# Loading the last weight matrix in pieces of 18, 6, 6, 4, 1 and 1 rows, and turning the last head's output ahead of the first piece's matmuls

## The chip, the cores and the metric

The kernel runs on one core of a Trainium2 chip. The metric is the device time of one execution in microseconds (us). Executions of the kernel before took 211.63 to 211.93 us in three runs, with a median of 211.7.

## The reference, cut to what matters

```python
def reference(A_x, A_k_cache, A_v_cache, A_wq, A_wo, B_x, B_w1, B_w2, B_w3, B_w4):
    # A: attention, one query token, 4 batches, 32 heads on 16 K/V heads, last 2048 keys, head size 128
    # ... q = xn @ wq, softmax, p @ v ...   then  o.reshape(B, 1, 4096) @ wo
    # B: an MLP. With one token, the shifted part of it contributes nothing but padding, so x1 = x:
    # h2 = gelu(layernorm(x1) @ w3) @ w4       w3: 576 x 4608, w4: 4608 x 576
    # B returns xn + h2; the whole result is 4 x 1 x 576
    ...
    xn = _layernorm(x, axis=-1)
    return x + _A_ref(xn, A_k_cache, A_v_cache, A_wq, A_wo) + _B_ref(xn, B_w1, B_w2, B_w3, B_w4)
```

The change touches the last product of each half: `gelu(...) @ w4`, and `o @ wo` for the last four K/V heads.

## The kernel before

Everything is read once from HBM in one queue, in the order wq, K and V of head after head (with wo and w3 between), and w4 last. w4 has 4608 rows; the kernel lays them out as 36 "rows" of 128 partitions by 576 columns and loads them in six pieces, each a DMA of its own with its own semaphore, so that matmuls of one piece can start while the next is on its way (in the trace of before rows 10 to 17 start at 202.05 us, and the next piece lands at 204.55).

```python
    W4_PIECES = [0, 10, NFH, NF - 6, NF - 2, NF - 1, NF]      # NF = 36, NFH = 18: 10, 8, 12, 4, 1, 1 rows

    def load_w4():
        t = wp.tile([P, NF, D], BF16, tag="w", name="w4_sb")
        for lo, hi in zip(W4_PIECES, W4_PIECES[1:]):
            e = lo // NFH
            src = B_w4[e * (F // 2):(e + 1) * (F // 2), :].rearrange("(p i) n -> p i n", i=NFH)
            nc.sync.dma_start(out=t[:, lo:hi, :], in_=src[:, lo - e * NFH:hi - e * NFH, :])
        w_tiles["w4"] = t
```

The results of both halves add up in one PSUM tile, `acc`. In the tail every second term goes to a second tile, `acc_odd`, at partitions from QD = 32 on, so that two matmuls stream at once (in the timeline the two of a pair start within 0.01 us of each other; those of a single row, both into `acc`, start 0.12 us apart):

```python
    def acc_matmuls(terms):
        for i in range(NI):                                   # NI = 2 halves of 288 columns
            for n, (lhsT, rhs) in enumerate(terms):
                to, q, start = (second[0], QD, second[1]) if second and n % 2 else (acc, 0, False)
                nc.tensor.matmul(out=to[q:q + OR, :], lhsT=lhsT[:, NI - 1 - i:NI - 1 - i + OR],
                                 rhs=rhs[:, i * CW:(i + 1) * CW], start=start, stop=False, skip_group_check=True)
                # ...

    def mlp_out(lo, hi):
        w4 = w_tiles["w4"]
        for i in range(lo, hi, 2):
            acc_matmuls([(gT[:, u, :], w4[:, u, :]) for u in range(i, min(i + 2, hi))])
```

The tail, in the order of TensorE's program. `o_turn` transposes a head's output on TensorE, `o_sum` folds it on VectorE, `o_spread` is eight small matmuls, `o_pick` two VectorE instructions, `o_proj` 16 matmuls with wo:

```python
    for s in range(NSL):
        pv(hl, s)
    o_scale(hl)                      # ScalarE, 0.69 us
    o_turn(hl - 1)
    o_sum(hl - 1)
    # ...
    mlp_out(*pieces[0])
    o_turn(hl)
    o_sum(hl)
    o_spread(hl)
    o_pick(hl)
    mlp_out(*pieces[1])
    o_proj(hl)
    mlp_out(*pieces[2])
    mlp_out(*pieces[3])
    second.clear()
    odd = const.tile([OR, CW], F32)
    nc.scalar.activation(out=odd[:], in_=acc_odd[QD:QD + OR, :], func=ACT.Copy)
    seen = const.tile([1, 1], F32)
    nc.vector.tensor_copy(out=seen[:], in_=odd[0:1, 0:1])
    for lo, hi in pieces[4:]:        # the two single rows, into acc alone
        mlp_out(lo, hi)
    fin = const.tile([OR, CW], out.dtype)
    nc.vector.tensor_tensor(out=fin[:], in0=acc[0:OR, :], in1=odd[:], op=ALU.add)
    nc.sync.dma_start(out=o2.rearrange("b (i n) -> (b i) n", i=NI), in_=fin[:])
```

## Time and profile before

| | before |
|---|---|
| time, median of the first 3 runs | 211.7 us |
| span of the profiled run | 209.8 us |
| DMA rate over the span | 416 GB/s |
| chain of waits: DMA, TensorE | 73%, 17% |
| last piece of w4 landed | 206.67 us |
| store of the result issued | 207.72 us |

In all views PE is TensorE, PEld its weight loads, DVE VectorE, ACT ScalarE, POOL GpSimd, and SP the engine that issues the DMAs (SPq its queue). The first lines are from the page of the kernel before: the span in 40 slices with the granted TensorE clock in tenths, the DMA engines' busy share in tenths and their rate; then the chain of waits by engine.

```profile
PEclk9999589696997556958999979997999985969999
DMA  8999999999999999999999999999999999999991
GB/s 301 400 419 431 434 428 419 439 428 425 445 429 427 423 431 425 449 419 431 440 422 434 434 409 444 434 428 423 444 414 437 418 450 419 434 428 421 434 409 69
...
DMA 73%; PE 17%; DVE 7%; ACT 1%; issue 1%; SPq 0%; DVEq 0%
```

The DMA engines are busy 90% or more of every slice from the second to the last but one. From this I took it, as an estimate, that a change that moves no bytes can act only after the last K/V work, in the final 10 us. Next, the DMA issues of that stretch (window 165 to 210 us): size, and time from issue to landing.

```profile
w_sb<-in_B_w_dram SPq DMA_DIRECT2D x1, 1728.0 KB, 34.6
w_sb<-in_B_w_dram SPq DMA_DIRECT2D x1, 1440.0 KB, 29.2
w_sb<-in_B_w_dram SPq DMA_DIRECT2D x1, 1152.0 KB, 31.3
w_sb<-in_B_w_dram SPq DMA_DIRECT2D x1, 576.0 KB, 31.2
w_sb<-in_B_w_dram SPq DMA_DIRECT2D x2, 144.0 KB, 24.4
```

All are issued 22 to 35 us before they land; the queue, not the issue, decides when: the last three are issued 4.85 and 4.90 us apart and land 0.35 and 0.37 us apart. With the issue times (168.4 to 184.5 us) the pieces land at 197.61, 200.35, 204.55, 205.95, 206.30 and 206.67 us. TensorE meets them like this (timeline: start, duration, engine and line, what; in brackets idle time and what ended it; most of the alternating matmuls left out):

```profile
199.41 0.29 PE L183 MATMUL acc<-w_sb,gT 128*8 128x288 bf16 x1
...
200.74 0.66 PE L403 MATMUL oT<-ident_w,O_sb 128*128 128x128 f32 x4
...
201.77 0.35 PE L422 MATMUL R<-on,sel_wo 128*128 128x32 bf16 x8 [0.38 <-DVE on L413]
...
203.10 0.29 PE L183 MATMUL acc<-wo_sb,op 128*8 128x288 bf16 x1
...
203.96 0.29 PE L183 MATMUL acc<-wo_sb,op 128*8 128x288 bf16 x1
...
204.59 0.28 PE L183 MATMUL acc<-w_sb,gT 128*8 128x288 bf16 x1 [0.34 <-DMA w_sb<-in_B_w_dram]
...
206.55 0.65 PE L183 MATMUL acc<-w_sb,gT 128*8 128x288 bf16 x4
206.75 0.40 ACT L606 ACTIVATE odd<-acc_odd 8x288 f32<-8x288 f32 x1 [7.07 <-PE acc_odd L183]
...
207.72 0.36 SPq L614 DMA_DIRECT2D out_dram<-fin  x1
```

Ten rows, the turn, a short wait for VectorE's sum, the spread, eight rows, the projection; then a wait of 0.34 us for the 12-row piece (the line at 204.59), and from there 18 rows in a row. Two rows take 0.24 us (two pairs, 0.12 us from start to start), a single one 0.24 too, as it has no partner.

### The profile page before, as it was taken

What the parts mean: (1) busy time and instruction counts of PE and PEld (TensorE: products, weight loads), DVE (VectorE), ACT (ScalarE), POOL (GpSimd) and SP (SyncE); (2) the same over time, 40 slices, a digit from 0 to 9 for tenths busy, and PEclk for the clock granted to TensorE, in tenths of its full rate; (3) what the DMA queues carried; (4) which work ended last, traced back from release to release, by engine and by line L of the source; (5) the groups of instructions that cost most, each with busy time, mean ns of one, the idle gap of its engine ahead of it and who ended that gap; (6) DMA issues with size and microseconds to landing.
All of it is one profiled execution on the core that took longest, in us unless ns stands there. A gap on an engine that the chain in (4) does not pass through costs nothing.

```text
span 209.8 us, 2403 instructions
## 1 busy us (share of the span) xinstructions
PE 149.1 (71%) x955; PEld 62.7 (30%) x955; DVE 120.4 (57%) x217; ACT 33.9 (16%) x64; POOL 2.8 (1%) x15
## 2 busy tenths in 40 slices
PE   0287496869691009659899599967994926989884
PEld 0133132223240003214364144332532401425353
DVE  3741899584840082825706878985399571771420
ACT  7602201020220000202102121120111110202300
POOL 4010000000000000000000000000000000000000
PEclk9999589696997556958999979997999985969999
DMA  8999999999999999999999999999999999999991
GB/s 301 400 419 431 434 428 419 439 428 425 445 429 427 423 431 425 449 419 431 440 422 434 434 409 444 434 428 423 444 414 437 418 450 419 434 428 421 434 409 69
DMA packets 6659, 87.32 MB, mean 416 GB/s; under 512 B 748, under 2 KB 1016, under 8 KB 1400
## 3 DMA queue, kind: packets, MB, share of 16 engines
q1 hardware_dynamic: 6640, 87.17, 97.5%
q8 instruction: 7, 0.11, 0.2%
q10 hardware_dynamic: 8, 0.00, 0.1%
q14 instruction: 4, 0.03, 0.0%
HBM read 87.17 MB, written 0.00 MB: 415 GB/s over the span
## 4 chain that ended last, share of the span: by engine, by line
DMA 73%; PE 17%; DVE 7%; ACT 1%; issue 1%; SPq 0%; DVEq 0%
DMA w_sb<-in_B_w_dram 33%; DMA vn<-in_A_v_cache_dram 24%; DMA wo_sb<-in_A_wo_dram 10%; DMA wq_sb<-in_A_wq_dram 6%; PE S L338 6%; DVE kt L225 4%; PE acc L183 3%; PE g_ps L456 2%; PE q_ps L285 2%; PE O L390 1%; PE oT L403 1%; DVE qz L317 1%; PE gT_ps L468 1%; DVE mx L344 1%; ACT q_sb L296 1%
## 5 line engine op out<-in xcount | busy, mean ns | idle before, releaser
L225 DVE STREAM_TRANSPOSE kt<-kn 128x1024 int32<-128x1024 int32 x64 | 76.5, 1216 | 12.4 <-DMA kn<-in_A_k_cache_dram 12.1
L338 PE MATMUL S<-kt,qz 128*128 128x512 bf16 x256 | 78.9, 437 | 3.1 <-DVE kt L225 3.1
L390 PE MATMUL O<-vn,PT 128*32 128x512 bf16 x256 | 27.2, 425 | 39.9 <-DMA vn<-in_A_v_cache_dram 38.1
L338 PEld LDWEIGHTS <-qz 128*128 128x128 bf16 x256 | 21.6, 103 | 41.1 <-issue 25.1
L366 ACT ACTIVATE E<-S 128x512 bf16<-128x512 f32 x16 | 9.6, 597 | 122.4 <-PE S L360 122.4
L390 PEld LDWEIGHTS <-PT 128*32 128x32 bf16 x256 | 7.2, 94 | 48.1 <-issue 29.6
L372 DVE STREAM_TRANSPOSE PT<-E 128x512 bf16<-128x512 bf16 x16 | 11.4, 710 | 15.3 <-ACT E L366 15.2
L397 ACT ACTIVATE O_sb<-O,rd 128x512 f32<-128x512 f32 x16 | 11.0, 686 | 15.8 <-issue 11.0
L356 DVE TENSOR_REDUCE nm<-mg 8x1 bf16<-8x16 f32 x16 | 2.4, 151 | 19.0 <-PE mg L351 19.0
L413 DVE TENSOR_REDUCE on<-oT 128x8 bf16<-128x128 f32 x16 | 4.5, 279 | 13.4 <-PE oT L403 13.4
L344 DVE TENSOR_REDUCE mx<-S 128x1 f32<-128x512 f32 x16 | 10.5, 657 | 1.3 <-PE S L338 1.3
L403 PE MATMUL oT<-ident_w,O_sb 128*128 128x128 f32 x64 | 11.2, 304 | 0.0
L403 PEld LDWEIGHTS oT<-ident_w,O_sb 128*128 128x128 f32 x64 | 9.1, 159 | 5.0 <-issue 3.2
L183 PE MATMUL acc<-wo_sb,op 128*8 128x288 bf16 x56 | 7.5, 286 | 0.0
L376 PEld LDWEIGHTS dn<-rs,same_j 128*128 128x128 f32 x32 | 5.8, 188 | 2.9 <-ACT E L366 0.7
L360 PE MATMUL S<-nm,j_row 8*128 8x512 bf16 x16 | 6.4, 402 | 0.0
L329 PE MATMUL S<-negbig,ohT 4*128 4x512 bf16 x16 | 6.2, 385 | 0.0
L183 PE MATMUL acc<-w_sb,gT 128*8 128x288 bf16 x38 | 5.1, 286 | 0.3 <-DMA w_sb<-in_B_w_dram 0.3
L183 PEld LDWEIGHTS <-op 128*8 128x8 bf16 x64 | 4.6, 87 | 2.5 <-issue 0.7
L351 PE MATMUL mg<-dm,sel_jb 128*8 128x16 bf16 x16 | 2.8, 174 | 3.6 <-DVE dm L346 3.5
L351 PEld LDWEIGHTS <-sel_jb 128*8 128x8 bf16 x16 | 1.3, 83 | 12.3 <-issue 5.6
L474 DVE COPY g_x<-gT_ps 128x64 f32<-128x64 f32 (+1 forms) x3 | 0.6, 193 | 7.7 <-PE gT_ps L468 7.7
(93 smaller groups left out, 84.6 us busy)
## 6 DMA issues: line engine op xcount, KB each, us to landing
kn<-in_A_k_cache_dram SPq DMA_DIRECT2D x16, 2048.0 KB, 22.0
vn<-in_A_v_cache_dram SPq DMA_DIRECT2D x16, 2048.0 KB, 24.4
wo_sb<-in_A_wo_dram SPq DMA_DIRECT2D x4, 1152.0 KB, 24.4
w_sb<-in_B_w_dram SPq DMA_DIRECT2D x1, 4608.0 KB, 34.0
wq_sb<-in_A_wq_dram SPq DMA_DIRECT2D x1, 4096.0 KB, 12.8
w_sb<-in_B_w_dram SPq DMA_DIRECT2D x1, 1728.0 KB, 34.6
w_sb<-in_B_w_dram SPq DMA_DIRECT2D x1, 1440.0 KB, 29.2
w_sb<-in_B_w_dram SPq DMA_DIRECT2D x2, 576.0 KB, 32.9
```

The source lines that it names most:

```text
L183: nc.tensor.matmul(out=to[q:q + OR, :], lhsT=lhsT[:, NI - 1 - i:NI - 1 - i + OR], rhs=rhs[:, i * CW:(i + 1) * CW], start=start, stop=False ...
L225: nc.vector.transpose(out=kt[:], in_=src)
L329: nc.tensor.matmul(out=S_ps[h][:].rearrange("p (c k) -> p c k", k=QD), lhsT=ohT[:], rhs=negbig[:].unsqueeze(1).to_broadcast([B, SC, QD]), ...
L338: nc.tensor.matmul(out=S_ps[h][:], lhsT=qz[:, z0:z0 + P], rhs=kt[:, ib, :, e:2 * QD:2].rearrange("p c k -> p (c k)"), start=False, stop=Fa ...
L344: nc.vector.reduce_max(out=mx[:], in_=S_ps[h][:], axis=AX.X)
L360: nc.tensor.matmul(out=S_ps[h][:], lhsT=j_row[:], rhs=st.pop(("nm", h))[:, 0:1].to_broadcast([NJ, NW]), start=False, stop=False, skip_grou ...
L366: nc.scalar.activation(out=E[h][:].rearrange("p c k -> p (c k)"), in_=S_ps.pop(h)[:], func=ACT.Exp, scale=scale, accum_out=rs[:])
L372: nc.vector.transpose(out=PT[h][:], in_=E.pop(h)[:])
L376: nc.tensor.matmul(out=dn[:], lhsT=same_j[:], rhs=st.pop(("rs", h))[:], start=True, stop=True)
L390: nc.tensor.matmul(out=O_ps[h][g * QD:(g + 1) * QD], lhsT=PT[h][:, c, :], rhs=vn[:, :, c, :], start=(s == 0), stop=False, skip_group_check ...
L397: nc.scalar.activation(out=O_sb[h][:], in_=O_ps.pop(h)[:], func=ACT.Copy, scale=st.pop(("rd", h))[:, 0:1])
L403: nc.tensor.transpose(out=oT[:, s, :], in_=o[:, s, :], identity=ident_w[:, s * NJ:s * NJ + P])
```

## The change

The intent is to fill the wait at 204.59. The first two pieces become one, the 12-row piece becomes two of six, so that rows 18 to 23 arrive on their own; and the last head's chain of turn, sum, spread and pick starts before the first piece's matmuls, so that VectorE's part hides behind 18 rows instead of 8.

```diff
-    W4_PIECES = [0, 10, NFH, NF - 6, NF - 2, NF - 1, NF]
+    W4_PIECES = [0, NFH, NF - 12, NF - 6, NF - 2, NF - 1, NF]
@@
-    mlp_out(*pieces[0])
     o_turn(hl)
     o_sum(hl)
     o_spread(hl)
     o_pick(hl)
+    mlp_out(*pieces[0])
+    o_proj(hl)
     mlp_out(*pieces[1])
-    o_proj(hl)
     mlp_out(*pieces[2])
     mlp_out(*pieces[3])
```

## The prediction

> **What bounds the kernel now.** The loads. The page's slices show the DMA engines at 0.8 or more up to the last slice, 416 GB/s over the span; [...] 429 GB/s in the stretch 170 to 190 us. The chain of waits is 73% DMA. The change moves no byte and adds no load: six pieces of w4 before, six after, issued by SP between 168.4 and 184.5 us, over 20 us before they land. Only the tail after about 199 us can change.
>
> **The tail before.** Issue times (timeline) plus times to landing (DMA issues) give the landings of the pieces (10, 8, 12, 4, 1, 1 rows): 197.6, 200.4, 204.55, 205.95, 206.3, 206.65 us. In the timeline TensorE runs ten rows at 199.41, turns the last head at 200.74, waits for VectorE's sum, starts the spread at 201.77, eight rows at 202.05, the projection at 203.10. It waits 0.3 us for the 12-row piece and starts it at 204.59, then streams 12+4+1+1 rows: two rows cost 2 x 0.12 us, a single row 0.24. Row 34 starts at 206.55, the last matmul near 206.9. Then ScalarE's copy (0.40), VectorE's probe and sum (0.14 + 0.43), the store at 207.72.
>
> **What the change does, costed.**
> 1. The turn comes first. It waits for ScalarE's scaled output (199.00 to 199.69), so it starts near 199.75, not 200.74. TensorE idles 0.3 us more there; turn to spread stays 1.03 us (spread near 200.8).
> 2. The 18 rows (landed by about 200.4) run from 201.1 to 203.25 (9 x 0.24 us), hiding VectorE's pick. Projection to about 204.25, as before.
> 3. Rows 18 to 23 land on their own by about 202.5 (estimate: half way between 200.4 and 204.55) and fill the wait, 204.25 to 205.0. Rows 24 to 29 (landed 204.55) run to 205.7. TensorE is about 0.35 us ahead.
> 4. But the 4-row piece still lands at 205.95: a new wait of about 0.25 us. Its rows take 0.48 us; row 34 starts near 206.47, row 35, whose piece lands at 206.65, near 206.72.
>
> So of 0.35 us won on TensorE about 0.08 survives; the last landings take the rest. Packets per load stay 128; one took 520 ns at 13,824 bytes and 178 at 4,608, so about 7 ns is fixed, and their number doesn't change: the last landing should not move.
>
> **Predicted time:** 211.6 us, against 211.7; 211.1 to 212.2 should hold it 8 times in 10 (the three runs before spread over 0.3). Faster by over 2%: 0.5%; within 2%: 99%; slower by over 2%: 0.5%.
>
> **What would show it.** Right: the turn near 199.75, spread near 200.8, no DMA wait before rows 18 to 29, a new TensorE wait of 0.1 to 0.4 us for the 4-row piece, the last piece landing within 0.3 us of 206.65, ScalarE's copy of the odd half 0 to 0.15 us earlier. Step 2 is wrong if TensorE waits for the 18-row piece; step 3 if the wait stands before rows 18 to 23; step 4 if row 34 starts over 0.2 us earlier.
>
> **What would make it wrong.** The last landings moving with the sizes ahead of them: [...] the postings for one piece spread over 1.8 us. If packet sizes change how far the slowest engine lags, the end moves by tenths of a microsecond either way. A lower granted clock in the tail (1.00 now) would add some.

## The result, and the profile after

| | runs | median | range | ratio to before, 95% interval |
|---|---|---|---|---|
| before | 6 | 211.75 us | 211.63 to 211.93 | |
| after | 6 | 211.93 us | 211.62 to 212.26 | 1.0007 (0.9993 to 1.0021) |

A ratio is the mean time of one kernel's runs over that of the other's of the same rounds, so it is not quite the ratio of the medians. The time is the same. The six runs of after fall into two groups: 211.62, 211.62, 211.70 and 212.16, 212.20, 212.26. The trace is of a run of the lower group.

The same lines of the page, after:

```profile
PEclk9999589696969556958999979997999985969999
DMA  7999999999999999999999999999999999999991
GB/s 301 400 412 437 428 428 428 436 422 428 469 408 420 433 428 427 438 431 428 431 437 428 422 425 446 425 425 436 422 436 428 421 435 440 425 425 448 418 402 72
...
DMA 72%; PE 18%; DVE 6%; ACT 1%; issue 1%; SPq 0%; DVEq 0%
```

The stream of loads is as it was. The issues (same window; the two six-row pieces share a line of 864 KB):

```profile
w_sb<-in_B_w_dram SPq DMA_DIRECT2D x1, 2592.0 KB, 31.9
w_sb<-in_B_w_dram SPq DMA_DIRECT2D x2, 864.0 KB, 33.9
w_sb<-in_B_w_dram SPq DMA_DIRECT2D x1, 576.0 KB, 31.1
w_sb<-in_B_w_dram SPq DMA_DIRECT2D x2, 144.0 KB, 24.4
```

The pieces land at 200.48, 202.55, 204.61, 206.00, 206.41 and 206.78 us: the boundary at row 18 and those from row 30 on are where they were, within 0.13 us. And TensorE's tail (timeline, same columns):

```profile
199.81 0.66 PE L403 MATMUL oT<-ident_w,O_sb 128*128 128x128 f32 x4 [0.26 <-ACT O_sb L397]
...
200.85 0.35 PE L422 MATMUL R<-on,sel_wo 128*128 128x32 bf16 x8 [0.38 <-DVE on L413]
...
201.13 0.29 PE L183 MATMUL acc<-w_sb,gT 128*8 128x288 bf16 x1
...
203.34 0.29 PE L183 MATMUL acc<-wo_sb,op 128*8 128x288 bf16 x1
...
204.32 0.29 PE L183 MATMUL acc<-w_sb,gT 128*8 128x288 bf16 x1
...
205.05 0.29 PE L183 MATMUL acc<-w_sb,gT 128*8 128x288 bf16 x1
...
205.66 0.29 PE L183 MATMUL acc<-w_sb,gT 128*8 128x288 bf16 x1
...
206.04 0.28 PE L183 MATMUL acc<-w_sb,gT 128*8 128x288 bf16 x1
...
206.53 0.70 PE L183 MATMUL acc<-w_sb,gT 128*8 128x288 bf16 x4
206.74 0.40 ACT L606 ACTIVATE odd<-acc_odd 8x288 f32<-8x288 f32 x1 [6.98 <-PE acc_odd L183]
...
207.74 0.37 SPq L614 DMA_DIRECT2D out_dram<-fin  x1
```

Rows 18 to 23 run at 204.32 and rows 24 to 29 at 205.05, without a wait. The last pair of row 29 starts at 205.66 and a pair takes 0.12, so the next could start near 205.79; the four-row piece starts at 206.04. That is the new wait, 0.25 us. The bracket shows none at 206.04, because each of these matmuls is recorded with 0.29 us, although the next pair starts 0.12 us after it. Counted from start to start in the same way, the wait before was not 0.34 but 0.51 us (the last pair of the projection starts at 203.96, so the next could start at 204.08). The chain of waits in order of time (start, duration, link) says it plainly. Before:

```profile
169.92 34.62 DMA w_sb<-in_B_w_dram
204.55 0.04 issue
204.59 0.28 PE acc L183
```

and after:

```profile
174.94 31.06 DMA w_sb<-in_B_w_dram
206.00 0.04 issue
206.04 0.28 PE acc L183
```

The last DMA of the chain was the 12-row piece, issued at 169.92; now it is the four-row piece, issued at 174.94. Row 34 starts at 206.53 instead of 206.55, the store at 207.74 instead of 207.72. The wait has moved 1.45 us towards the end, and nothing came out at the end.

### The profile page after: what moved, and what is told of

It is laid out like the page before. It is cut to its first block, busy times and chain, and to the rows that moved or that the text cites. A ratio compares the mean times of both kernels' runs of the same rounds, so it can differ in the third digit from the quotient of the medians. Undisturbed runs are those within 1.5% of the kernel's fastest.

```text
span 209.8 us, 2403 instructions
## 1 busy us (share of the span) xinstructions
PE 149.9 (71%) x955; PEld 62.8 (30%) x955; DVE 120.4 (57%) x217; ACT 33.9 (16%) x64; POOL 2.8 (1%) x15
## 4 chain that ended last, share of the span: by engine, by line
DMA 72%; PE 18%; DVE 6%; ACT 1%; issue 1%; SPq 0%; DVEq 0%
DMA vn<-in_A_v_cache_dram 35%; DMA w_sb<-in_B_w_dram 31%; PE S L338 7%; DMA wq_sb<-in_A_wq_dram 6%; DVE kt L225 3%; PE acc L183 2%; PE g_ps L456 2%; PE q_ps L285 2%; PE O L390 2%; PE oT L403 1%; DVE qz L317 1%; PE gT_ps L468 1%; DVE mx L344 1%; PE S L360 1%; ACT q_sb L296 1%
## 5 line engine op out<-in xcount | busy, mean ns | idle before, releaser
L338 PE MATMUL S<-kt,qz 128*128 128x512 bf16 x256 | 79.7, 441 | 3.1 <-DVE kt L225 3.1
L338 PEld LDWEIGHTS <-qz 128*128 128x128 bf16 x256 | 21.7, 104 | 41.5 <-issue 25.8
```

Of the source, the lines that this page charges most:

```text
L338: nc.tensor.matmul(out=S_ps[h][:], lhsT=qz[:, z0:z0 + P], rhs=kt[:, ib, :, e:2 * QD:2].rearrange("p c k -> p (c k)"), start=False, stop=Fa ...
```

## The experiments

Theory T: the landings of the last pieces set the end; what TensorE wins earlier, it waits away there. Rivals: the amount of TensorE's work in the tail is the bound; or the new order costs what the new sizes win. Kernels of one table shared a chip and the runs of before.

| kernel | runs (us) | median | ratio to before, 95% interval |
|---|---|---|---|
| before | 11: 211.51 to 211.81, one 212.28 | 211.71 | |
| e1_after_again | 211.58, 212.46, 211.43, 211.76, 211.44, 211.68 | 211.63 | 0.9999 (0.9983 to 1.0014) |
| e2_order_only | 211.77, 211.59, 212.39, 211.59, 211.64, 211.56 | 211.62 | 1.0000 (0.9985 to 1.0015) |
| e3_sizes_only | 214.15, 213.90, 213.89, 212.82, 212.28, 212.24 | 213.35 | 1.0069 (1.0040 to 1.0098) |
| e8_split_four | 211.95, 212.65, 212.73, 211.60, 211.81, 212.71 | 212.30 | 1.0023 (1.0004 to 1.0042) |

| kernel | runs (us) | median | ratio to before, 95% interval |
|---|---|---|---|
| before | 11: 211.53 to 211.94 | 211.71 | |
| e4_after_no_proj | 211.40, 211.51, 211.65, 211.41, 211.77 | 211.51 | 0.9993 (0.9981 to 1.0004) |
| e5_before_no_proj | 213.10, 213.97, 211.67, 211.72, 211.62, 214.00 | 212.41 | 1.0046 (1.0009 to 1.0083) |
| e6_after_no_last6 | 211.73, 212.87, 213.11, 212.94, 211.76, 211.98 | 212.43 | 1.0039 (1.0019 to 1.0059) |
| e7_before_no_last6 | 212.76, 212.29, 212.29, 212.47, 212.42 | 212.42 | 1.0035 (1.0023 to 1.0047) |

| kernel | runs (us) | median | ratio to before, 95% interval |
|---|---|---|---|
| before | 11: 211.50 to 211.90 | 211.68 | |
| e9_filled | 211.62, 211.63, 211.77, 211.76, 211.56 | 211.63 | 1.0000 (0.9988 to 1.0011) |
| e10_after_third | 213.12, 211.71, 211.56, 212.41, 211.48, 211.44 | 211.63 | 1.0002 (0.9988 to 1.0016) |
| e11_filled_again | 211.54, 211.56, 211.75, 211.60, 211.49 | 211.56 | 0.9996 (0.9984 to 1.0008) |
| e12_after_fourth | 211.80, 211.48, 211.73, 211.82, 211.48 | 211.73 | 0.9999 (0.9987 to 1.0011) |

The first run of each list is the profiled one.

### e1_after_again: the control

No edit.

> The changed kernel again, as the control of this chip. Theory T (the landings of the last pieces set the end, and what TensorE wins earlier is spent waiting for them): ratio to before within 0.9990 to 1.0025, no DMA wait of TensorE before rows 18 to 29, one of 0.2 to 0.4 us before the four-row piece. The first result had runs at 211.6 to 211.7 and others at 212.2 to 212.3 us; if those two levels are of the kernel, they come again in this kernel and not in before; if of the chip or of chance, before or the other kernels of this call show them too.

Measured: ratio 0.9999; TensorE's tail as in the first trace, the last piece landed at 206.73 and the store left at 207.71. One run of six was at 212.46, and one of the eleven of before at 212.28. The high level is not of this kernel alone, but it is more frequent here; more below.

### e2_order_only: the new order, the old sizes

```diff
 # against after
-    W4_PIECES = [0, NFH, NF - 12, NF - 6, NF - 2, NF - 1, NF]
+    W4_PIECES = [0, 10, NFH, NF - 6, NF - 2, NF - 1, NF]
```

> New order of TensorE's work, old sizes (10, 8, 12, 4, 1, 1). T: the turn near 199.8 and the spread near 200.85 as in the changed kernel, but the wait stays before the twelve-row piece (about 0.3 us, landing near 204.55), the rest of the tail as before; ScalarE's copy of the odd half at 206.75 within 0.1 us, time within 0.1 us of before. Rival (the new idle time ahead of the turn, 0.26 us, is what cancels a gain): slower than before by 0.2 to 0.3 us.

Measured: ratio 1.0000. The interval reaches to 0.3 us slower, so the time alone does not exclude the rival's 0.2 to 0.3; the trace does, for this run: the idle time ahead of the turn (0.26 us) comes before a wait of 1.67 us, and row 34 and the store follow the landing of the 12-row piece as in before. But two numbers were not as expected. The turn was at 198.39, not near 199.8, and the wait at the 12-row piece 1.67 us, not 0.3. TensorE had come into the tail 1.4 us earlier than in the traces of before and after, and spent it there. The page's clock records explain it: in the traces of before and after the granted clock was 0.5 from 184.8 or 185.0 to 188.2 or 188.4 us, just ahead of the tail, and in this one it was 1.0 from 179.7 on.

```profile
198.39 0.66 PE L403 MATMUL oT<-ident_w,O_sb 128*128 128x128 f32 x4 [0.26 <-ACT O_sb L397]
...
204.73 0.28 PE L183 MATMUL acc<-w_sb,gT 128*8 128x288 bf16 x1 [1.67 <-DMA w_sb<-in_B_w_dram]
```

The last 16 score matmuls (L338) start at 184.88 in before and at 185.05 here, and the last of them at 194.03 and 192.67: the whole difference arises in that stretch. (In before, the L338 matmuls of one group start 0.42 us apart at the clock of 0.5 and 0.23 us apart at 1.0.) So the kernel comes into its tail "late" or "early", by whether that stretch of half clock lies just ahead of it (the page's slice from 184 to 189 us has the clock digit 6 in before and after, and 9 in the early e3, e4, e5 and e10), and a reading of slack from one trace holds for one of the two. Of these traces before, after, e1, e7, e9, e11 and e12 are late, the rest early.

### e3_sizes_only: the new sizes, the old order

```diff
 # against before
-    W4_PIECES = [0, 10, NFH, NF - 6, NF - 2, NF - 1, NF]
+    W4_PIECES = [0, NFH, NF - 12, NF - 6, NF - 2, NF - 1, NF]
```

> New sizes (18, 6, 6, 4, 1, 1), old order: the eighteen rows ahead of the turn. T: TensorE waits about 1.0 us at 199.4 for the eighteen-row piece (landing near 200.4), turn near 202.7, spread near 203.7, projection done near 205.7, then TensorE is the bound: rows 24 to 35 run without a wait, last matmul near 207.3, 0.3 to 0.5 us slower than before. Rival (the last landing alone sets the end, whatever TensorE does): within 0.1 us of before.

Measured: in the right direction, but about four times as much at the median: 212.24 to 214.15 us. The lower three runs lie 0.5 to 1.1 us above before, the upper three 2.2 to 2.4. In the profiled run, one of the upper three, TensorE waited 2.48 us for the 18 rows (it was early, too), and then this happened (a stretch and its length; busy time of PE, PEld, DVE, ACT and POOL with their instructions; the granted clock, the DMA share and rate):

```profile
197.60:201.00 3.40, 0.92 (x12) 0.67 (x12) 0.29 (x1) 0.66 (x1) 0.00 (x0) 1.00 0.95 395
201.00:204.40 3.40, 3.40 (x32) 1.89 (x26) 0.00 (x0) 0.00 (x0) 0.00 (x0) 0.50 0.99 409
```

TensorE was busy 0.92 of 3.40 us, and for the next 3.4 us its clock was halved (0.50), just while it had to run the 18 rows (pairs 0.24 us apart from 201.05 on, 0.12 before). The turn then came at 204.51, and the projection, which has to follow it, at 206.87. The clock records of before and after hold 1.0 and 0.5 and no other value, and every stretch of theirs but the last, which the end of the trace cuts off, is 3.413 us long or a multiple of that (up to 23.893 us); the stretch here is of 3.4 us. T's sum had left this term out. The rival "the last landing sets the end, whatever TensorE does" falls: the last piece landed at 206.76, as ever, and the store left at 210.26. So the merged first piece is affordable only together with the new order.

### e8_split_four: removing the new wait

```diff
 # against after
-    W4_PIECES = [0, NFH, NF - 12, NF - 6, NF - 2, NF - 1, NF]
+    W4_PIECES = [0, NFH, NF - 12, NF - 6, NF - 4, NF - 2, NF - 1, NF]
@@
     mlp_out(*pieces[3])
+    mlp_out(*pieces[4])
     second.clear()
@@
-    for lo, hi in pieces[4:]:
+    for lo, hi in pieces[5:]:
```

> The changed kernel with the four-row piece in two of two rows (18, 6, 6, 2, 2, 1, 1). T: two rows land near 205.3, so the 0.3 us wait at the four-row piece goes, and ScalarE's copy starts 0.2 to 0.3 us earlier, but row 35 still waits for its landing near 206.7: the last matmul and the time 0 to 0.1 us earlier than the changed kernel. Rival (the wait for the four-row piece is the only bound): 0.25 us earlier.

Measured: not faster (median 212.30, three runs of six at 212.65 to 212.73, which have no trace; the others 211.60 to 211.95). In the trace the last piece landed at 206.98, its matmuls followed, and the store left 0.96 us after that landing, exactly as in after. No 0.25 us appeared, so the wait at the four-row piece was not the only bound: behind it stands the landing of row 35 (0.20 us later here than in after). ScalarE's copy was not earlier either (206.75), because the second pair of rows landed at 206.26.

### e4_after_no_proj and e5_before_no_proj: taking TensorE work away

Both results are wrong: the last projection is missing. (The comparison with the reference still passed; its tolerance is wider than this term.)

```diff
 # e4, against after
     mlp_out(*pieces[0])
-    o_proj(hl)
     mlp_out(*pieces[1])
 # e5, against before
     mlp_out(*pieces[1])
-    o_proj(hl)
     mlp_out(*pieces[2])
```

> The changed kernel without the last projection (16 matmuls, 0.97 us of TensorE; the result is wrong on purpose). T: TensorE waits longer for DMA (before rows 18 to 23 or 24 to 29, and at the four-row piece), the four-row piece starts at the same time within 0.1 us, time unchanged within 0.1 us. Rival (the amount of TensorE work in the tail is the bound): 0.7 to 1.0 us faster.

Measured: ratio 0.9993; the interval reaches from 0.4 us faster to 0.1 slower, so the rival's 0.7 to 1.0 us is excluded. The timeline shows where the 0.97 us went (all three lines are waits for pieces of w4):

```profile
200.34 0.28 PE L183 MATMUL acc<-w_sb,gT 128*8 128x288 bf16 x1 [0.75 <-DMA w_sb<-in_B_w_dram]
...
204.47 0.28 PE L183 MATMUL acc<-w_sb,gT 128*8 128x288 bf16 x1 [1.03 <-DMA w_sb<-in_B_w_dram]
...
205.87 0.28 PE L183 MATMUL acc<-w_sb,gT 128*8 128x288 bf16 x1 [0.50 <-DMA w_sb<-in_B_w_dram]
```

TensorE now waits three times, for rows 0, 24 and 30, and starts the four-row piece 0.04 us after its landing (205.83), as after did (206.00 and 206.04).

> The kernel before without the last projection (wrong on purpose). T: TensorE's wait before the twelve-row piece grows from 0.3 to about 1.3 us, nothing after 204.6 moves, time within 0.1 us of before. Rival: 0.7 to 1.0 us faster.

Measured: three runs at 211.62 to 211.72, as T says, and three at 213.10 to 214.00. Less work, and up to 2.3 us slower. The profiled run is one of the slow three:

```profile
200.90:204.30 3.40, 0.82 (x14) 0.46 (x11) 0.63 (x2) 0.00 (x0) 0.00 (x0) 1.00 0.96 397
204.30:207.70 3.40, 3.12 (x28) 1.82 (x29) 0.00 (x0) 0.00 (x0) 0.00 (x0) 0.50 0.35 132
```

The wait before the 12-row piece had grown to 2.86 us, the clock fell to a half from 204.3 to 207.7, and until then the rows behind the wait ran at half speed (pairs 0.24 us apart, against 0.12 in before). The landings were those of every run (last 206.65).

### e6_after_no_last6 and e7_before_no_last6: taking the late landings away

Wrong: rows 30 to 35 are not loaded, and their matmuls read rows 0 to 5.

```diff
-        for lo, hi in zip(W4_PIECES, W4_PIECES[1:]):
+        for lo, hi in list(zip(W4_PIECES, W4_PIECES[1:]))[:3]:
@@
-            acc_matmuls([(gT[:, u, :], w4[:, u, :]) for u in range(i, min(i + 2, hi))])
+            acc_matmuls([(gT[:, u, :], w4[:, u % (NF - 6), :]) for u in range(i, min(i + 2, hi))])
```

> The changed kernel without the loads of the last six rows (their matmuls read rows 0 to 5 instead; wrong on purpose), so the late landings are gone and the TensorE work stays. T: no wait after rows 24 to 29, rows 30 to 35 run on from 205.8, ScalarE's copy and the last matmul 0.25 to 0.35 us earlier than in the changed kernel. Rival (TensorE's work is the bound): no gain.

> The kernel before without the loads of the last six rows (wrong on purpose). T: TensorE still waits for the twelve-row piece (landing near 204.55) and then runs without a break, as it nearly did before, so the time is within 0.1 us of before; the changed kernel without these loads is 0.25 to 0.4 us faster than this one, the gain that its late landings hide. Rival (the two orders are equally fast on TensorE): the two are equal within 0.1 us.

Measured in the traces: without the late pieces, after's store left at 207.10, 0.64 us before that of after with them; before's left at 208.17. From the landing of row 29 to the store it is 2.44 us in e6 (204.66 to 207.10) and 3.18 us in e7 (204.99 to 208.17), where before itself has 3.17 (204.55 to 207.72). So before gains nothing when the late pieces go, and after gains 0.7 us from that landing on, which is what six rows cost TensorE (six times 0.12). That is the hidden gain; I had expected 0.25 to 0.4 from a late trace, and e6's trace is an early one, in which all six rows are done before row 29 lands.

Measured in times: a miss. Both kernels are slower than before, not equal or faster, and their medians (212.43 and 212.42) are equal, as the rival said. The traces show two things that T had not counted. In both, more time passes between the store's issue and the end of the run: 2.83 us in e6 and 2.81 in e7, against 2.08 to 2.11 in every trace with six pieces of w4 (and 2.23 in e8, with seven). The second drain of SP after the store starts 0.78 us after the result has landed (in e6 208.34 and 209.12), against 0.15 in before; what held it, the records do not show. That cancels e6's 0.64 us. And in e7 the loads from about 110 us on are 0.3 to 0.55 us later than in before, long before the missing pieces. Neither of these was followed up, and e6's upper three runs (212.87 to 213.11) have no trace. The two kernels show T in the order of events, not in the time.

### e9_filled to e12_after_fourth: what the high runs are

```diff
 # e9 and e11, against after; e10 and e12 are after without an edit
     o_turn(hl)
+    for _ in range(5):
+        nc.tensor.matmul(out=acc_odd[2 * QD:2 * QD + OR, :], lhsT=gT[:, 0, 0:OR],
+                         rhs=wo_tiles[hl // WOQ][:, 0, 0:CW], start=True, stop=False, skip_group_check=True)
     o_sum(hl)
     o_spread(hl)
```

> The changed kernel with five spare matmuls (128x8 by 128x288 into an unused quadrant of the odd half's bank, about 0.6 us, correct result) between the last head's turn and its spread, where TensorE waits 0.65 us for VectorE in every trace. Question: the changed kernel had runs at 212.2 to 212.5 in 4 of 12, its other runs at 211.4 to 211.8. Theory C (in those runs a window of low TensorE use in the tail halves its granted clock for the next window of 3.4 us): with the idle time filled the high level is gone or rare (0 or 1 of 6), the rest unchanged at 211.4 to 211.8, spread not later than 0.1 us. Rival (the high level has nothing to do with TensorE's idle time): about 2 of 6 runs above 212.

> The changed kernel once more, as the control of the filled one. Both theories: about 2 of 6 runs above 212, the rest at 211.4 to 211.8. If the profiled run is one of the high ones: theory C expects a granted clock of 0.5 in a stretch between 199 and 208 us in its trace; the rival a clock of 1.0 there and later landings, or later ends after the store.

> The filled kernel again, for the count of high runs and a second trace. Theory C: 0 or 1 of 6 above 212; rival: about 2 of 6.

> The changed kernel a fourth time, for the count and one more trace. Both: about 2 of 6 above 212; if the profiled run is high, theory C expects a granted clock of 0.5 somewhere between 199 and 208 us, the rival 1.0 throughout.

Measured: the spare matmuls delayed the spread by 0.26 us, not by 0.1 at most (turn to spread 1.30 us in both filled traces, 1.04 in after): the wait that they were to fill is 0.38 us by the bracket, and the 0.65 of the expectation counts from the start of the turn's last matmul. The changed kernel had 6 of 23 runs above 212 us, before 1 of 39, the filled kernel 0 of 10. The profiled run of e10 was a high one, 213.12 us. Its stretches and its tail:

```profile
198.00:201.40 3.40, 1.97 (x24) 1.38 (x22) 1.43 (x4) 0.69 (x1) 0.00 (x0) 1.00 0.94 395
201.40:204.80 3.40, 3.40 (x32) 2.09 (x30) 0.00 (x0) 0.00 (x0) 0.00 (x0) 0.50 0.98 399
204.80:208.20 3.40, 3.40 (x58) 2.60 (x55) 0.00 (x0) 0.00 (x0) 0.00 (x0) 1.00 0.24 89
```

```profile
201.23 0.29 PE L183 MATMUL acc<-w_sb,gT 128*8 128x288 bf16 x1 [0.79 <-DMA w_sb<-in_B_w_dram]
...
208.04 0.65 PE L183 MATMUL acc<-w_sb,gT 128*8 128x288 bf16 x4
...
209.22 0.37 SPq L614 DMA_DIRECT2D out_dram<-fin  x1
```

Two things came together. The last landing was at 207.49, about 0.7 us later than in the other traces, and the 18-row piece was late as well (201.19). And TensorE, early and waiting 0.79 us for that piece, was busy only 1.97 of 3.40 us and got half the clock from 201.4 to 204.8, so that it ran without a break from there to the end and the store left 1.73 us after the last landing instead of 0.97. By this subtraction (an estimate) each is worth about 0.75 us, together the 1.5 us above the low runs. The same wait does not always cost the clock: e4, e6 and e8 waited 0.75 to 0.79 us for that piece too, and kept 1.0; the clock windows of 3.413 us that hold those waits were busy for 2.10 us or more. Theory C's clock is thus shown for this run; that it makes all the high runs is not. The runs at 212.2 to 212.5 have no trace, and the late landing alone would explain that level too. Nor is the filled kernel's 0 of 10 proof: with a true share of 6 in 23, ten runs without one are to be expected in about one case in twenty (17/23 to the tenth power), and both its traces are late ones, in which after did not lose the clock either. It is not faster than before (1.0000 and 0.9996), so no version here beats both kernels.

## Why the prediction was right

The time lay in the range. That alone proves little: the expected gain of 0.1 us is 0.05% of the time. The median of the six runs lies 0.3 us above the predicted 211.6, because three of them were high ones, which the prediction did not foresee; one, 212.26, lies above the range. That the median did not is partly luck; over all 23 runs of the changed kernel it is 211.70. What carries the prediction is its order of events. The best single view is how long after the last landing the store leaves:

| trace | last landing | store issued | between |
|---|---|---|---|
| before | 206.67 | 207.72 | 1.06 |
| after | 206.78 | 207.74 | 0.96 |
| e1_after_again | 206.73 | 207.71 | 0.99 |
| e2_order_only | 206.84 | 207.86 | 1.02 |
| e4_after_no_proj | 206.55 | 207.54 | 0.99 |
| e8_split_four | 206.98 | 207.94 | 0.96 |
| e9_filled, e11_filled_again | 206.76, 206.71 | 207.75, 207.68 | 0.99, 0.97 |
| e12_after_fourth | 206.97 | 207.93 | 0.96 |
| e5_before_no_proj, half clock | 206.65 | 209.22 | 2.57 |
| e3_sizes_only, half clock | 206.76 | 210.26 | 3.49 |
| e10_after_third, half clock | 207.49 | 209.22 | 1.73 |

(Computed from unrounded times.) In every trace with the last six rows loaded and a full clock in the tail, whatever its order, its sizes or its amount of TensorE work, the store follows the last landing by 0.96 to 1.06 us. By order and sizes there was 0.1 us at most to win here, and after has it: 0.96 against 1.06. Its last landing happened to be 0.11 us later.

The same records say more exactly what bounds the end. In all nine of these traces the store leaves, within 0.01 us, at the latest of three times: 3.175 us after the landing of the 12-row piece (this one decides in before and e2, where TensorE then runs 18 rows without a break), 1.705 us after that of the four-row piece (through ScalarE's copy; e1, e4 and e9), and 0.957 us after the last landing (after, e8, e11 and e12). In before the first lies 0.07 and 0.10 us beyond the other two. So the change takes away the bound that decided, and with before's landings that would be worth 0.07 us, close to the 0.08 of the prediction. (The three distances were read from these same traces.)

Point by point:

- "What bounds the kernel now. The loads." Right; e4 takes 0.97 us of TensorE work away and the time stays.
- Step 1, the turn near 199.75 and the spread near 200.8: 199.81 and 200.85.
- Step 2, the 18 rows from 201.1 without a wait: right in the late traces of the changed kernel (201.13 in after; e1 and e12 show no such wait either), wrong in the early one: in e10 TensorE waited 0.79 us for the 18-row piece, and the early variants e4, e6 and e8 waited 0.75 to 0.79. The prediction took its slack from one trace, and there are two modes 1.4 us apart.
- Step 3, rows 18 to 29 without a DMA wait: right in after (204.32 and 205.05). Rows 18 to 23 were estimated to land at 202.5 and landed at 202.55. TensorE was 0.27 us ahead at the end of row 29 (its last pair at 205.66, in before at 205.93), not 0.35.
- Step 4, "a new wait of about 0.25 us" at the four-row piece: 0.25. Row 34 was to start at 206.47 and started at 206.53, as the piece landed at 206.00 instead of 205.95. So of the surviving 0.08 us, 0.02 was seen in this pair of traces, and none of it can be seen in the times.
- "The last landing should not move": 206.67 to 206.78, within the 206.55 to 206.98 of all the other traces that load every piece, except e10. The working beside it is rough: the 520 ns is a mean, with one packet of 994; the other 127 took 516, which leaves about 9 ns fixed, not 7.
- "A lower granted clock in the tail (1.00 now) would add some": it does, in e10 (0.50 from 201.4 to 204.8), by about 0.75 us (the estimate above), and the merged 18-row piece is what TensorE waited for there. That the change makes such runs more frequent (6 of 23 against 1 of 39) fits, but which of the two causes made the others is open.

## What to carry to other kernels

Here the last landings set the end, and finer pieces and a better order in front of them only moved the wait, by 1.45 us towards the end; the store left 0.96 us after the last landing, against 1.06. In another kernel, find the last landing, measure from there to the store, and work on that distance or on the bytes. Before judging slack from one trace, look at whether TensorE comes early or late in others; here a stretch of half clock just ahead of the tail (185.0 to 188.4 us in before) shifted it by 1.4 us. A wait that costs nothing by itself can still be followed by half the clock for the next 3.4 us (in e5 a wait of 2.86 us, TensorE busy 0.82 of 3.40 us, then a granted clock of 0.50): removing TensorE work ahead of a wait came with half of the runs being 1.4 to 2.3 us slower (the one that was profiled had the halved clock).

## What the traces show of the clock, of the postings and of the end

- The clock fell to a half after short waits: TensorE was busy 1.97 of 3.40 us in e10, with a longest marked wait of 0.79 us, and had half the clock (0.50) in the following 3.4 us. With 0.92 (e3) and 0.82 (e5) of 3.40 us it was the same. Cut into windows of 3.413 us at the changes of the granted clock, the 14 traces hold 133 windows (from 10 us on) after which a full clock fell to half; none of them was busy for more than 2.15 us (in before there are 9, the busiest 1.96 us; in after 10, the busiest 2.08). Windows from 1.60 to 2.15 us were followed by either.
- In before the 16 postings of one load (the updates of its semaphore in the trace) spread over 0.47 us at 28 us and over 1.86 us at 31 us, where the trace has an instruction fetch of 16,384 bytes at 30.6 us taking 0.88 us; after the later fetches (for example at 105, 124 and 142 us) the following loads show one more late posting each (3 of the 16 come over 0.8 us after the first in the load at 104 us, 4 at 109, 5 at 126 and 6 at 146), and the spread stays at 1.6 to 1.9 us to the end. In e10 the last posting fell from 1.8 to 2.8 us behind the first between the loads that landed at 147.7 and 163.2 us; this is its late last landing. A fetch stands between them, at 154.6 us, but before has one at 155.0 us without such a fall. No experiment here took a fetch away, so the cause is inferred.
- The time from the store's issue to the end of the program was not the same with all loads: it was 2.08 to 2.11 us with six pieces of w4, 2.23 with seven (e8), and 2.81 to 2.83 with three (e6 and e7).
